# Retention's scores and transposes as quarter-array products, two pacing constants, and the order of the last retention step

## The chip, the cores and the metric

The kernel runs on one core of a Trainium2 chip. The metric is the device time of one execution in microseconds. TensorE does the matrix products, VectorE and ScalarE empty its result banks, GpSimd does a few elementwise steps, SyncE issues most transfers.

## What is computed

Three layers follow each other: a retention over 4 batches of 8 heads with 576 positions and head size 64, then a layer with a mish-like gate (512 to 2048 to 512), then a layer with a SiLU gate (512 to 1536 to 512). Tokens: 4 x 576 = 2304.

```python
scores = scale * np.matmul(q, k.transpose(0, 1, 3, 2))
Dmat = np.where(rel >= 0, gamma[:, None, None] ** rel[None, :, :], 0.0)
ret = scores * Dmat[None, :, :, :]
attn = np.matmul(ret, v)
...
h = x @ w_in
sp = np.where(h > 20.0, h, np.log1p(np.exp(np.minimum(h, 20.0))))
x = (h * np.tanh(sp)) @ w_out
...
g = x @ w_gate
silu = g * (1.0 / (1.0 + np.exp(-g)))
out = (silu * (x @ w_val)) @ w2_out
```

## The kernel before, in words

Every engine executes its instructions in the order in which the program writes them.

**Retention** (`retention`, lines 441 to 799) runs 20 steps: four batches, each of four chunks of 128 positions and one of 64. In a step `scores` (line 601) multiplies keys by queries into the bank tile `s`, one product for each of 8 heads; VectorE multiplies by the mask into `p` (line 616). Then `turn` (line 509) transposes what the next steps need: the keys of the next step (`k_item`) and a part of the queries of a later one (`q_item`, chosen by `q_next`). ScalarE copies the results out of the bank. Then `output` (line 672) adds three things: the carried state times queries (line 685), the update of the state (`state`, line 650) and masked scores times scaled values (line 700). ScalarE copies the state out (`state_out`, line 664) and VectorE multiplies the output by a decay into `x` (line 713). In eight of the steps (`EARLY`) `g1` puts one product of the next layer (line 808, bank `h`) between line 685 and line 650.

A head has 64 columns, so these products fill a part of the array of 128 rows and 128 columns. The trace gives the part as rows*columns: scores stand as 64*128 (two in the array at a time, one for each half of the rows), line 685 as 64*64 (four at a time), lines 650 and 700 as 128*64 (two at a time). The transposes come in two kinds. `halves` (line 493) uses the transpose operation on 64 rows and 128 columns, one product for each; `quarters` (line 499) multiplies by the identity on 64 rows and 64 columns, and the trace shows two products for each such call, as it does for all other float32 calls of this stage. Keys need quarters for odd pairs of heads, full query chunks (`whole`) use halves alone. The chunk of 64 positions uses only the upper half of the rows. At the start of batch 0 the queries of steps 2 and 3 are transposed inside step 1 (`q0_1` by ScalarE, `q0_1b` by VectorE).

**First gated layer** (lines 1139 to 1189). For the last part `pair1` runs seven block products for each of eight pairs of columns, twice. The block products of one pair share two banks, emptied by ScalarE and VectorE; the line of a block product is 965, the line of the second matmul that is put between them is 1020. Beside this, `second`, a `Pace` object (line 396), emits the preparation of the third layer's weights (VectorE lines 133, 137, 228, 238, 276, with ScalarE casts and transfers). Each call adds a rate to an allowance and emits pieces while the allowance covers their costs. `RATES[2]` is the rate in the middle of a run, `RATES[4]` the rate of the last eleven block products. What is left at the end is emitted at once by `second(1000.0)`, ahead of the second gated layer (`strassen`, line 1243), whose block products use line 965 too, in tile `t`.

Of the kernel before, what the change touches and what calls it, by code (L numbers as in the profile page):

```python
# [17 lines left out]
def retention_mish_swiglu(  # L18
# [17 lines left out]
    nc = tc.nc  # L36
# [5 lines left out]
    NP = H // 2  # L42
# [4 lines left out]
    RAW, XS = 4, 6  # L47
    W = (12, 3, 3)
    NC = 2
    RATES, AHEAD = (0.8, 1.2, 1.37, 0.95, 1.05), 45  # L50
    EARLY = (8, 10, 11, 13, 14, 16, 17, 19)
    FIRSTS = (0, 2, 1, 3, 4, 5, 6, 7)
    REST, NO_FETCH = (1, 3, 6, 18), (2, 5)
# [381 lines left out]
    steps = []  # L435
# [5 lines left out]
    def retention(g1, mish, g_hi, g_lo):  # L441
        with ExitStack() as c0:
# [6 lines left out]
            ident = cp.tile([128, 128], F32, tag="ident", name="ident")  # L449
# [33 lines left out]
            qT, kT, vs, pp = {}, {}, {}, {}  # L483
# [5 lines left out]
            def row(pr, e):  # L489
                r = 64 * (e ^ pr % 2)  # L490
                return slice(r, r + 64)

            def halves(n, src, to, pairs):
                for pr in pairs:
                    for r in range(-(-n // 64)):
                        own = slice(64 * r, min(64 * r + 64, n))
                        nc.tensor.transpose(to(r, pr)[:, :own.stop - own.start], src(pr)[own], ident[own, own])  # L497

            def quarters(n, src, to):
                for pr in range(1, NP, 2):  # L500
                    for e in range(2):
                        for r in range(-(-n // 64)):
                            own = slice(64 * r, min(64 * r + 64, n))
                            nc.tensor.matmul(  # L504
                                to(r, pr)[row(pr, e), :own.stop - own.start], lhsT=src(pr)[own, e, :],
                                rhs=ident[own, own], start=True, stop=True, skip_group_check=True,
                            )

            def turn(name, *items, tag="tt", both=False):
                items = [x for x in items if x]  # L510
                if not items:
                    return
                p = ps1.tile([128, 2, 2, NP, 64], F32, tag=tag, name=f"t{name}")
                to = [lambda r, pr, z=z: p[:, r, z, pr] for z in range(2)]
                for z, (n, src, _, whole) in enumerate(items):
                    halves(n, src, to[z], range(0, NP, 1 if whole else 2))
                for z, (n, src, _, whole) in enumerate(items):
                    if not whole:
                        quarters(n, src, to[z])
                for z, (_, _, empty, _) in enumerate(items):  # L520
                    if not both:
                        empty(p[:, :, z])
                        continue
                    for r, copy in enumerate((nc.scalar.copy, nc.vector.tensor_copy)):
                        empty(p[:, :, z], r, copy)


            def first_k():
                n, src, *_ = k_item(0)
                p = [ps1.tile([128, NP, 64], F32, tag=tag, name=f"tk0_{tag}") for tag in ("o", "st")]  # L530
                halves(n, src, lambda r, pr: p[r][:, pr], range(0, NP, 2))
                quarters(n, src, lambda r, pr: p[r][:, pr])
                kT[0] = at.tile([128, NP, 128], F32, tag="kT", name="kT0")
                for r, copy in enumerate((nc.scalar.copy, nc.vector.tensor_copy)):
                    copy(out=kT[0][:, :, 64 * r:64 * r + 64], in_=p[r])
# [43 lines left out]
            def q_cols(t):  # L579
                b, sc, n = steps[t]  # L580
                return qT[b, sc // 2][:, :, sc % 2 * 128:sc % 2 * 128 + n]
# [19 lines left out]
            def scores(t):  # L601
                b, sc, n = steps[t]
                s = ps1.tile([128, 2, NP, 128], F32, tag="s", name=f"s{t}")
                for pr in range(NP):
                    for e in range(2):
                        nc.tensor.matmul(  # L606
                            s[:n, e, pr, :n],
                            lhsT=kT[t][64 * e:64 * e + 64, pr, :n],
                            rhs=q_cols(t)[64 * e:64 * e + 64, pr],
                            start=True,  # L610
                            stop=True,
                        )
                pp[t] = at.tile([128, 2, NP, 128], F32, tag="p", name=f"p{t}")
                for c in range(2):
                    own = slice(c * NP // 2, (c + 1) * NP // 2)
                    nc.vector.tensor_tensor(
                        out=pp[t][:n, :, own, :n],
                        in0=s[:n, :, own, :n],
                        in1=mask[:n, :n].unsqueeze(1).unsqueeze(1).to_broadcast([n, 2, NP // 2, n]),
                        op=ALU.mult,  # L620
                    )
# [37 lines left out]
            def state_out(t):  # L659
                b, sc, n = steps[t]  # L660
                if sc == nsc - 1:
                    return
                if sc < nsc - 2:
                    nc.scalar.copy(out=sd, in_=stp[b])
                    return
                for e in range(2):
                    for m in range(2):
                        nc.scalar.copy(
                            out=sbd[row(m, e), m::2, 64 * e:64 * e + 64], in_=stp[b][row(m, e), m::2, :],
                        )  # L670

            def output(t):
                b, sc, n = steps[t]

                o = ps1.tile([128, 2, 512], F32, tag="o", name=f"o{t}")
                o = o.rearrange("p b (a n) -> p b a n", n=128)

                def place_of(pr, e):
                    return o[64 * e:64 * e + 64, pr % 2, pr // 2, :n]

                if sc:
                    for pr in range(NP):
                        for e in range(2):
                            own = row(pr, e)
                            nc.tensor.matmul(  # L685
                                place_of(pr, e),
                                lhsT=sd[own, pr, :] if n == 128 else sbd[:, pr, 64 * e:64 * e + 64],
                                rhs=q_cols(t)[own, pr] if n == 128 else q_cols(t)[:, pr],
                                start=(pr < 2), stop=False, skip_group_check=True,
                            )  # L690
                if t in EARLY:
                    g1(FIRSTS[EARLY.index(t)])
                state(t)
                if t == 1:
                    turn("q0_1", q_item(0, 1, 0))
                    turn("q0_1b", q_item(0, 1, 1, nc.vector.tensor_copy), tag="s")
                state_out(t)
                for pr in range(NP):
                    for e in range(2):
                        nc.tensor.matmul(  # L700
                            place_of(pr, e),
                            lhsT=vs[t][:n, 2 * pr + e, :],
                            rhs=pp[t][:n, e ^ pr % 2, pr, :n],
                            start=(sc == 0 and pr < 2), stop=True, skip_group_check=True,
                        )
                t0 = b * S + sc * 128
                done = 0
                while done < n:
                    j, off = divmod(t0 + done, T)
                    m = min(n - done, T - off)  # L710
                    if j not in xt:
                        new_x(xt, j, "x")
                    nc.vector.tensor_tensor(
                        out=xt[j][:, :, off:off + m].rearrange("p (a b) n -> p b a n", b=2),
                        in0=o[:, :, :NP // 2, done:done + m],
                        in1=gout[:, :, sc * 128 + done:sc * 128 + done + m].rearrange("p (a b) n -> p b a n", b=2),
                        op=ALU.mult,
                    )
                    done += m
                    if j < 2 and off + m == T:  # L720
                        due.extend((j, kk) for kk in range(KT))
# [79 lines left out]
    with tc.manual_schedule():  # L801
# [15 lines left out]
        def g1(s):  # L817
            i, b = divmod(s, NC)
            hs[s] = h_bank(f"h{s}")
            prod(hs[s], unit["in", i], "x", b)  # L820
# [326 lines left out]
        for i in range(inside, F1):  # L1147
            for b in range(NC):
                s = NC * i + b
# [270 lines left out]
        for k, (load, steps_) in enumerate(more):  # L1420
            side[0, 2 * k, 0, 6 * k] = [load]
            if k == 0:
                at_ = [(0, 1, 0, c) for c in range(NG)] + [(0, 1, 1, c) for c in range(4)] + [(0, 2, 0, c) for c in range(3)]
# [76 lines left out]
```

## Time and profile before

| what | value |
|---|---|
| median of three runs | 878.18 us (878.05 to 879.94) |
| the profiled execution's own time | 878.28 us |
| its span (first to last instruction) | 876.5 us |
| TensorE busy | 869.0 us, 99% of the span |
| VectorE busy | 641.6 us, 73% |
| ScalarE busy | 429.7 us, 49% |
| GpSimd busy | 48.6 us, 6% |

The span and the 1.8 us around it make the profiled time. Retention fills the first 102 us of the span, the first gated layer reaches to about 464 us. In the timeline a row is a group of neighbouring instructions of one line; its first number is when the first of them starts, its second how long the group lasts, and the ends of matmuls are modelled, so the text takes differences between starts.

### The profile page before, as it was taken

How to read it: one execution, taken by the hardware profiler on the slowest of the kernel's cores; microseconds unless marked ns; L12 is line 12 of the kernel's file. 1: busy time of each engine (PE TensorE's matmuls, PEld its weight loads, DVE VectorE, ACT ScalarE, POOL GpSimd, SP SyncE). 2: the span in 40 equal slices, each digit the busy share in tenths (PEclk: the TensorE clock that was granted, in tenths of full speed). 3: DMA queues.
4: the chain of work that ended last, by engine and by line, in shares of the span. 5: the costliest groups of instructions: out<-in, count | busy, mean ns of one | idle time of the engine just before them, and what ended most of it. 6: DMA issues, size and time to landing. Idle time of an engine off the chain costs nothing.

```text
span 876.5 us, 17164 instructions
## 1 busy us (share of the span) xinstructions
PE 869.0 (99%) x6570; PEld 830.4 (95%) x6570; DVE 641.6 (73%) x1260; ACT 429.7 (49%) x842; POOL 48.6 (6%) x46
## 2 busy tenths in 40 slices
PE   8999999999999999999999999999999999999998
PEld 8888899999999999999998999999999999999998
DVE  4678688887887876878695877975676776575773
ACT  3667367776665655656664342363222263222260
POOL 3554200000000000000000000000000000000000
PEclk9999999999999999999999999999999999999999
DMA  9999647886799985999977799878877878777773
GB/s 214 227 252 222 204 138 261 284 319 214 246 341 315 333 288 189 313 340 335 305 272 282 257 359 306 276 248 297 272 250 248 249 255 285 279 252 249 248 248 128
DMA packets 162850, 232.25 MB, mean 265 GB/s; under 512 B 48336, under 2 KB 126672, under 8 KB 162768
## 3 DMA queue, kind: packets, MB, share of 16 engines
q1 hardware_dynamic: 161232, 230.33, 81.7%
q8 instruction: 52, 0.85, 0.4%
q10 hardware_dynamic: 1536, 0.82, 0.4%
q14 instruction: 30, 0.25, 0.1%
HBM read 178.68 MB, written 52.43 MB: 264 GB/s over the span
## 4 chain that ended last, share of the span: by engine, by line
PE 92%; DVE 4%; DMA 2%; ACT 1%; issue 1%; SPq 0%; POOL 0%; DVEq 0%; ACTq 0%; POOLq 0%
PE t L965 30%; PE T L1386 15%; PE te L965 12%; PE h L808 8%; PE e0a L1020 8%; PE pa L1020 8%; PE e1a L1020 5%; PE s L606 2%; PE o L700 2%; PE state L650 1%; DMA v<-in_v_dram 1%; PE t L504 1%; DMA fcomb<-c 1%; PE o L685 1%; DVE y L920 1%; PE t L497 1%
## 5 line engine op out<-in xcount | busy, mean ns | idle before, releaser
L965 PE MATMUL t<-y,su 128*128 128x384 f32 x1512 | 267.9, 337 | 1.1 <-DVE scratch L972 0.8
L965 PEld LDWEIGHTS t<-y,su 128*128 128x128 f32 x1512 | 264.1, 188 | 3.5 <-DVE scratch L972 1.1
L965 PE MATMUL te<-ye,eu 128*128 128x384 f32 x672 | 135.9, 337 | 0.0
L1386 PE MATMUL T<-su,g 128*128 128x256 f32 x1134 | 135.3, 282 | 0.0
L1386 PEld LDWEIGHTS T<-su,g 128*128 128x128 f32 x1134 | 135.2, 190 | 0.0
L965 PEld LDWEIGHTS te<-ye,eu 128*128 128x128 f32 x672 | 113.1, 188 | 4.7
L1020 PE MATMUL e1a<-ge,u 128*128 128x512 f32 (+1 forms) x384 | 76.1, 337 | 0.0
L1020 PE MATMUL e0a<-ge,u 128*128 128x512 f32 (+1 forms) x384 | 76.1, 337 | 0.0
L808 PE MATMUL h<-xs,u 128*128 128x384 f32 x384 | 72.8, 338 | 0.0
L1020 PE MATMUL pa<-g,u 128*128 128x512 f32 (+1 forms) x384 | 72.2, 336 | 0.0
L1020 PEld LDWEIGHTS e1a<-ge,u 128*128 128x128 f32 x384 | 61.9, 188 | 6.0
L1020 PEld LDWEIGHTS e0a<-ge,u 128*128 128x128 f32 x384 | 62.0, 188 | 5.9
L808 PEld LDWEIGHTS h<-xs,u 128*128 128x128 f32 x384 | 65.3, 188 | 2.1 <-issue 0.9
L1020 PEld LDWEIGHTS pa<-g,u 128*128 128x128 f32 x384 | 60.5, 188 | 6.7
L1255 ACT ACTIVATE sg<-sg 128x384 f32<-128x384 f32 x54 | 28.4, 526 | 57.3 <-DVE sg L972 57.3
L1284 ACT COPY p<-t 128x384 f32<-128x384 f32 x35 | 16.6, 473 | 81.0 <-PE t L965 81.0
L1216 ACT CAST g<-ga 128x384 fp32r<-128x384 f32 x72 | 32.6, 517 | 44.1 <-DVE ga L1263 33.4
L972 DVE TENSOR_TENSOR u<-t,p 128x384 f32<-128x384 f32 x36 | 20.1, 557 | 40.9 <-PE t L965 40.9
L975 DVE TENSOR_TENSOR g<-ga,g 128x384 fp32r<-128x384 f32 x72 | 36.2, 551 | 6.4 <-ACT g L1216 6.2
L972 DVE TENSOR_TENSOR scratch<-te,scratch 128x384 f32<-128x384 f32 x48 | 26.6, 554 | 7.6 <-PE te L965 4.3
L972 DVE TENSOR_TENSOR v<-t,p 128x384 f32<-128x384 f32 x36 | 20.1, 557 | 15.9 <-PE t L965 15.8
L1063 ACT ACTIVATE ve<-ve 128x384 f32<-128x384 f32 x16 | 8.4, 527 | 45.7 <-DVE ve L972 45.7
(194 smaller groups left out, 1190.1 us busy)
## 6 DMA issues: line engine op xcount, KB each, us to landing
su<-comb SPq DMA_DIRECT2D x126, 512.0 KB, 4.3
su<-fcomb SPq DMA_DIRECT2D x63, 512.0 KB, 4.3
eu<-ecomb SPq DMA_DIRECT2D x56, 512.0 KB, 5.8
comb<-c SPq DMA_DIRECT2D x48, 256.0 KB, 5.2
raw<-in_moe_w_in_dram SPq DMA_DIRECT2D x16, 512.0 KB, 5.2
raw<-in_moe_w_out_dram SPq DMA_DIRECT2D x16, 512.0 KB, 5.7
ecomb<-e SPq DMA_DIRECT2D x32, 256.0 KB, 4.7
ecomb<-u SPq DMA_DIRECT2D x24, 256.0 KB, 4.6
```

The costliest lines, as they stand in the source:

```text
L497: nc.tensor.transpose(to(r, pr)[:, :own.stop - own.start], src(pr)[own], ident[own, own])
L606: nc.tensor.matmul(s[:n, e, pr, :n], lhsT=kT[t][64 * e:64 * e + 64, pr, :n], rhs=q_cols(t)[64 * e:64 * e + 64, pr], start=True, stop=True,)
L700: nc.tensor.matmul(place_of(pr, e), lhsT=vs[t][:n, 2 * pr + e, :], rhs=pp[t][:n, e ^ pr % 2, pr, :n], start=(sc == 0 and pr < 2), stop=Tru ...
L808: nc.tensor.matmul(ps, lhsT=u[:, a, kk * 128:(kk + 1) * 128], rhs=s[:, e, :], start=(c == 0), stop=(c == n - 1),)
L965: nc.tensor.matmul(p, lhsT=w[:, (high, 1 - high)[a], kk * 128:(kk + 1) * 128], rhs=y[kk][:, x, :], start=begin and kk == 0 and (a, x) == ( ...
L972: nc.vector.tensor_tensor(out=out_, in0=a, in1=b_, op=ALU.add)
L975: nc.vector.tensor_tensor(out=out_, in0=a, in1=b_, op=ALU.subtract)
L1020: nc.tensor.matmul(o, lhsT=unit["out", f][:, a, d * 128:(d + 1) * 128], rhs=y[:, :512] if r == 0 else y[:, 512:], start=f == 0 and (a, x) ...
L1216: nc.scalar.copy(out=gt[n, c, i][:, 0], in_=x)
L1255: nc.scalar.activation(x, bank_ if part_ is None else x, AF.Silu)
L1284: (nc.scalar.copy if n or i or z else nc.vector.tensor_copy)(out=r["p1"], in_=p)
L1386: nc.tensor.matmul(p[m], lhsT=g[:, x, m * 128:(m + 1) * 128], rhs=w[:, 1 - a, :], start=begin and i == 0 and (a, x) == (0, 0) and not (sha ...
```

## The change

Three edits. Scores are cut into pieces of 64 key columns, so that four stand in the array at a time, and all transposes are quarters; the function for halves is gone. In the last of the 20 steps `g1` comes ahead of the state's products; in step 1 `state_out` is written behind line 700's products. Two rates of the pacing change.

```diff
-    RATES, AHEAD = (0.8, 1.2, 1.37, 0.95, 1.05), 45
+    RATES, AHEAD = (0.8, 1.2, 1.42, 0.95, 0.95), 45
...
-            def halves(n, src, to, pairs):
-                for pr in pairs:
-                    for r in range(-(-n // 64)):
-                        own = slice(64 * r, min(64 * r + 64, n))
-                        nc.tensor.transpose(to(r, pr)[:, :own.stop - own.start], src(pr)[own], ident[own, own])
-
-            def quarters(n, src, to):
-                for pr in range(1, NP, 2):
+            def quarters(n, src, to, whole):
+                for pr in range(NP):
                     for e in range(2):
+                        at_ = slice(64 * e, 64 * e + 64) if whole else row(pr, e)
                         for r in range(-(-n // 64)):
                             own = slice(64 * r, min(64 * r + 64, n))
                             nc.tensor.matmul(
-                                to(r, pr)[row(pr, e), :own.stop - own.start], lhsT=src(pr)[own, e, :],
+                                to(r, pr)[at_, :own.stop - own.start], lhsT=src(pr)[own, e, :],
                                 rhs=ident[own, own], start=True, stop=True, skip_group_check=True,
                             )
...
                 for z, (n, src, _, whole) in enumerate(items):
-                    halves(n, src, to[z], range(0, NP, 1 if whole else 2))
-                for z, (n, src, _, whole) in enumerate(items):
-                    if not whole:
-                        quarters(n, src, to[z])
+                    quarters(n, src, to[z], whole)
...
                 for pr in range(NP):
-                    for e in range(2):
-                        nc.tensor.matmul(
-                            s[:n, e, pr, :n],
-                            lhsT=kT[t][64 * e:64 * e + 64, pr, :n],
-                            rhs=q_cols(t)[64 * e:64 * e + 64, pr],
-                            start=True,
-                            stop=True,
-                        )
+                    for c in range(0, n, 64):
+                        for e in range(2):
+                            nc.tensor.matmul(
+                                s[c:c + 64, e, pr, :n],
+                                lhsT=kT[t][64 * e:64 * e + 64, pr, c:c + 64],
+                                rhs=q_cols(t)[64 * e:64 * e + 64, pr],
+                                start=True, stop=True, skip_group_check=True,
+                            )
...
+                if t + 1 == len(steps):
+                    g1(FIRSTS[EARLY.index(t)])
                 if sc:
...
-                if t in EARLY:
+                if t in EARLY and t + 1 < len(steps):
                     g1(FIRSTS[EARLY.index(t)])
                 state(t)
...
-                state_out(t)
+                if t != 1:
+                    state_out(t)
...
+                if t == 1:
+                    state_out(t)
```

The orders below give instructions by line, written tile, read tiles and output size; a call counts once, and line numbers behind the edits are lower by 4 to 9 in the changed kernel.

On TensorE, step 6, a full chunk with keys (`k`) and a whole query part (`q`) to transpose, before:

```order
L606 MATMUL s_709<-qT_0_521,kT_671 128x128 x8
L497 MATMUL t_721<-ident,k_563 128x64 x4
L497 MATMUL t_721<-ident,q_488 128x64 x8
L504 MATMUL t_721<-ident,k_563 64x64 x8
L685 MATMUL o_751<-qT_0_521,sd 64x128 x8
L650 MATMUL state_680<-vs_676,k_490 64x64 x8
```

And the same step of the changed kernel:

```order
L598 MATMUL s_833<-qT_0_613,kT_795 64x128 x16
L499 MATMUL t_853<-ident,k_655 64x64 x16
L499 MATMUL t_853<-ident,q_562 64x64 x16
L678 MATMUL o_895<-qT_0_613,sd 64x128 x8
L641 MATMUL state_804<-vs_800,k_564 64x64 x8
```

Eight score calls become 16, and 12 halves with 8 quarters become 32 quarters; from the scores to line 685 all calls have one shape of tile.

On TensorE, the last step (scores `s`, the layer's product `h`, the state's part and the rest of the output `o`), before:

```order
L606 MATMUL s_1791<-qT_2_1655,kT_1752 64x64 x8
L685 MATMUL o_1804<-qT_2_1655,sbd 64x64 x8
L808 MATMUL h_1813<-xs_0_853,u_1256 128x384 x3
L808 MATMUL h_1813<-xs_1_943,u_1256 128x384 x3
L808 MATMUL h_1813<-xs_2_1022,u_1256 128x384 x3
L808 MATMUL h_1813<-xs_3_1111,u_1256 128x384 x3
L700 MATMUL o_1804<-p_1800,vs_1754 64x64 x8
```

And now:

```order
L598 MATMUL s_2127<-qT_2_1975,kT_2088 64x64 x8
L804 MATMUL h_2141<-xs_0_1011,u_1498 128x384 x3
L804 MATMUL h_2141<-xs_1_1119,u_1498 128x384 x3
L804 MATMUL h_2141<-xs_2_1210,u_1498 128x384 x3
L804 MATMUL h_2141<-xs_3_1319,u_1498 128x384 x3
L678 MATMUL o_2140<-qT_2_1975,sbd 64x64 x8
L694 MATMUL o_2140<-p_2136,vs_2090 64x64 x8
```

The 12 products of `h` stand between the scores and the state's part, which is now followed at once by the rest of the output.

On VectorE, the end of the first gated layer, behind its last-but-one block product (`scratch` and `ge` belong to the block products, `y` to the next layer's input, `c` and `rawf` to the weights that `second` prepares, `p_0_0` to the next layer's first block product), before:

```order
L920 TENSOR_TENSOR y_5_1_5601<-t_0_5424,y_5_1_5601 128x384
L228 TENSOR_TENSOR c_0_5529<-c_0_5529 128x512
L972 TENSOR_TENSOR scratch<-te_7_3_5560,scratch 128x384
L1070 TENSOR_TENSOR ge_15_5571<-scratch,ge_15_5571 128x384
L920 TENSOR_TENSOR y_6_0_5606<-y_3116,y_6_0_5606 128x384
L920 TENSOR_TENSOR y_6_1_5607<-y_3116,y_6_1_5607 128x384
L228 TENSOR_TENSOR c_1_5556<-c_1_5556 128x512
L228 TENSOR_TENSOR rawf_0_5323<-rawf_0_5323 128x256
L1284 COPY p_0_0_5663<-t_0_0_1_5656 128x384
```

And now:

```order
L916 TENSOR_TENSOR y_5_1_5947<-t_0_5771,y_5_1_5947 128x384
L968 TENSOR_TENSOR scratch<-te_7_3_5909,scratch 128x384
L1066 TENSOR_TENSOR ge_15_5920<-scratch,ge_15_5920 128x384
L916 TENSOR_TENSOR y_6_0_5952<-y_3452,y_6_0_5952 128x384
L916 TENSOR_TENSOR y_6_1_5953<-y_3452,y_6_1_5953 128x384
L1280 COPY p_0_0_5999<-t_0_0_1_5992 128x384
```

The three pieces of line 228 stand earlier now, ahead of the addition `ve_7` of the fifth block product of that pair. On the queue of SyncE the transfers of prepared weights and of `su` and `eu` tiles are moved past each other in the same stretch.

## Rows read from the trace of the kernel before

**Rows 1.** The page: busy us, share of the span, instructions of each engine.
```profile
PE 869.0 (99%) x6570; PEld 830.4 (95%) x6570; DVE 641.6 (73%) x1260; ACT 429.7 (49%) x842; POOL 48.6 (6%) x46
```

**Rows 2.** TensorE's waits: who waited for whom, total us, times, longest.
```profile
PE t L965 <- DVE scratch L972: 0.8, 1, 0.8
...
PE o L700 <- DVE p L616: 0.3, 1, 0.3
```

**Rows 3.** Timeline, TensorE, step 6: start, us, engine, line, tiles, array part, output, count.
```profile
33.74 1.16 PE L606 MATMUL s<-qT,kT 64*128 64x128 f32 x16
34.73 0.28 PE L497 MATMUL t<-ident,k 64*128 64x64 f32 x4
...
35.20 0.46 PE L504 MATMUL t<-ident,k 64*64 64x64 f32 x16
35.48 0.62 PE L685 MATMUL o<-qT,sd 64*64 64x128 f32 x16
36.03 0.69 PE L650 MATMUL state<-vs,k 128*64 128x64 f32 x16
```

**Rows 4.** Timeline, TensorE, step 12: keys, then the short query chunk.
```profile
64.36 0.29 PE L497 MATMUL t<-ident,k 64*128 64x64 f32 x4
...
64.98 0.35 PE L504 MATMUL t<-ident,q 64*64 64x64 f32 x6
...
65.21 0.61 PE L685 MATMUL o<-qT,sd 64*64 64x128 f32 x14
```

**Rows 5.** Timeline, TensorE, step 13: short key chunk, then a whole query part.
```profile
68.24 0.22 PE L497 MATMUL t<-ident,k 64*128 64x64 f32 x1
...
68.98 0.61 PE L685 MATMUL o<-qT,sd 64*64 64x128 f32 x14
```

**Rows 6.** Timeline, TensorE, step 14, a chunk of 64 positions.
```profile
73.29 0.68 PE L606 MATMUL s<-qT,kT 64*64 64x64 f32 x16
73.90 0.34 PE L497 MATMUL t<-ident,k 64*128 64x64 f32 x4
...
74.81 0.69 PE L685 MATMUL o<-qT,sbd 128*64 128x64 f32 x16
```

**Rows 7.** Timeline, step 1's query transposes and their copies, then step 2.
```profile
15.82 0.46 PE L497 MATMUL tq<-ident,q 64*128 64x64 f32 x8 [0.16 <-DMA q<-in_q_dram]
...
16.46 1.09 PE L700 MATMUL o<-p,vs 128*64 128x128 f32 x16
16.57 1.40 DVE L554 COPY qT<-tq_1b 64x512 f32<-64x512 f32 x2 [1.14 <-PE tq_1b L497]
...
18.11 1.16 PE L606 MATMUL s<-qT,kT 64*128 64x128 f32 x16 [0.55 <-ACT sd L664]
...
19.51 0.34 PE L497 MATMUL t<-ident,q 64*128 64x64 f32 x2
```

**Rows 8.** Timeline, TensorE, the last step: scores and the state's part.
```profile
97.53 0.68 PE L606 MATMUL s<-qT,kT 64*64 64x64 f32 x16
98.48 0.69 PE L685 MATMUL o<-qT,sbd 128*64 128x64 f32 x16 [0.27 <-DVE x L713]
```

**Rows 9.** Timeline, end of the first gated layer, TensorE and one row of VectorE.
```profile
460.16 1.20 PE L1020 MATMUL e1a<-ge,u 128*128 128x512 f32 x6
...
462.26 1.21 PE L1020 MATMUL e1a<-ge,u 128*128 128x512 f32 x6
...
463.68 0.55 DVE L972 TENSOR_TENSOR scratch<-te,scratch 128x384 f32<-128x384 f32 x1
...
464.28 1.32 PE L965 MATMUL t<-y,su 128*128 128x384 f32 x6 [0.81 <-DVE scratch L972]
...
465.44 1.61 PE L1020 MATMUL e1a<-ge,u 128*128 128x512 f32 x8
...
468.25 1.56 PE L1020 MATMUL e1a<-ge,u 128*128 128x512 f32 x8
```

**Rows 10.** Timeline, VectorE, a piece of `second` that waits for a transfer.
```profile
438.38 0.43 DVE L238 TENSOR_TENSOR c<-c,rawf 128x256 f32<-128x256 f32 x1 [1.81 <-DMA fcomb<-c]
```

More of the change, by code (lines that the diff above doesn't have):

```diff
@@ L530, in first_k @@
                 p = [ps1.tile([128, NP, 64], F32, tag=tag, name=f"tk0_{tag}") for tag in ("o", "st")]
-                halves(n, src, lambda r, pr: p[r][:, pr], range(0, NP, 2))
-                quarters(n, src, lambda r, pr: p[r][:, pr])
+                quarters(n, src, lambda r, pr: p[r][:, pr], False)
                 kT[0] = at.tile([128, NP, 128], F32, tag="kT", name="kT0")
```

## The prediction

> **What bounds the kernel now.** I read three views in this order. The page first: TensorE is busy for 869.0 of 876.5 us [rows 1], so a change counts only by what it does to TensorE's own work or to its few waits. Then the list of TensorE's waits: little stands in it, and the two rows that touch this change are 0.8 us of line 965 for a VectorE addition and 0.3 us of line 700 for masked scores [rows 2]. Last the timeline of single retention steps, where the reader should look at the distances from one row's start to the next: they repeat to 0.01 us from step to step, since TensorE is seldom waited out. Retention is therefore a sum of TensorE pieces, and the change replaces pieces.
>
> **The paces.** All sums rest on four numbers.
> - A set of products with 64 output columns costs 0.058 us, whether two or four stand in the array: 8 products of a short query chunk, two abreast, take 0.23 us from 64.98 to 65.21 [rows 4].
> - Four sets of four take 0.28 us from 35.20 to 35.48 [rows 3], which is 4 x 0.058 and 0.05 for the start after the tile form has changed.
> - A set with 128 output columns costs 0.11 us in either form: scores take 0.99 us for 8 sets of two, line 685 takes 0.55 us for 4 sets of four [rows 3], and the difference is four sets.
> - Halves cost 0.03 us each, and a change of form 0.10 us: 12 halves take 0.47 us from 34.73 to 35.20 [rows 3].
>
> **Scores.** Cutting them in two doubles the products (16 to 32) and the number abreast, so there are still 8 sets. What is saved is the longer start: 0.99 becomes 8 x 0.11 + 0.05 = 0.93, that is -0.06 in each of 16 full steps, -1.0 together. In the short chunks nothing is cut, but the following transposes have the same form now: 0.61 [rows 6] becomes 8 x 0.058 + 0.05 = 0.51, three times -0.10.
>
> **Transposes.** A call of `halves` is one product for a 64x128 block; as quarters it is four products. The keys' and whole queries' transposes of a step (0.75 us from 34.73 to 35.48 [rows 3]) become 64 products in 16 sets of 0.058, 0.93 us: +0.18 in six steps, +1.1. Steps with a short query chunk (0.85 us, 64.36 to 65.21 [rows 4]) also come to 0.93: +0.08, four times, +0.3. Steps with a short key chunk (0.74 us, 68.24 to 68.98 [rows 5], and 0.01 of line 685 that ran under it) come to 0.93 and lose that overlap: +0.20, three times, +0.6. Behind a chunk of 64 (0.91 us, 73.90 to 74.81 [rows 6]) it is 0.93 and one change of form, 0.10: +0.13, three times, +0.4. Keys alone get 0.03 cheaper (0.12 + 0.10 + 0.28 against 0.47) in two steps and at the head. The query transposes of step 1 (0.64 us, 15.82 to 16.46 [rows 7]) are 16 halves; as 64 products with start and change of form they take 1.09, +0.45, and the same pattern stands once more at the head: +0.9. Together the transposes cost +3.2, and scores and transposes +1.9 us of TensorE time.
>
> **What hides some of it.** In step 1 the transposes wait for a query load (0.16 us [rows 7]), so about 0.2 us of what came before costs nothing. Step 2's scores do not wait for TensorE but for the copies of step 1's transposes: VectorE starts them at 16.57, takes 1.40, and scores start at 18.11 [rows 7]. With the transposes 0.45 later this wait stays and all moves by 0.45, as summed. In step 2 the short query chunk's transposes start at 19.51, some 0.3 later than 18.11 + 0.99 + 0.12, waiting for a load; the longer key transposes now fill that. In steps 5 and 6 line 700 waits for VectorE's masking (0.3 us [rows 2] and shorter ones beside it), which takes +0.12 of each. Sum hidden: 0.75 us. If a load came later than here, its wait would return and the cover be smaller.
>
> **The last step.** Scores run from 97.53 and the state's part starts at 98.48, 0.95 us later, because VectorE still reads the output bank [rows 8]; the same 16 products take 0.61 before the next row in step 14 [rows 6]. With the next layer's 12 products in between, that 0.34 us goes. They write another bank and wait for nothing that is late there. Moving step 1's `state_out` changes the order on no engine (ScalarE copies the same things in the same order): 0.
>
> Retention thus becomes 1.9 - 0.75 - 0.34 = +0.8 us longer.
>
> **The pacing.** Before the second gated layer TensorE runs 6 and 6 products in 2.10 us (460.16 to 462.26), 0.175 each. The next 12 take 3.18 (to 465.44), the 14 after them 2.81 instead of 2.45 (to 468.25): 1.08 + 0.36 = 1.44 us lost [rows 9]. The row at 464.28 names the cause: it needs a bank that VectorE's addition at 463.68 frees, over 3 us after its block product, and the order shows weight pieces of line 228 in front of that addition and of the copy behind it. The new rates emit 0.05 more in each of 73 calls and 0.1 less in each of the last 11 (counted in the code of `pair1`), 2.55 units of allowance earlier, so these pieces lie ahead of the last three block products. VectorE has idle time earlier to take them (it even stood 1.81 us for a transfer at 438 [rows 10]). I take -1.3 of the 1.44; bounds are 0 and -1.44.
>
> **Sum.** 878.28 + 0.8 - 1.3 = 877.8 us by the profiled execution, which stands 0.10 above the median of the runs, so **877.7 us**. Its own range, from a set at 0.055 instead of 0.058 (half of a 128-column set; 288 sets, -0.9) and from hidden time that is not hidden (+0.75), is 876.7 to 878.7.
>
> **Rivals.** 0.2% or 1.8 us is about what a measurement of this kernel can tell from no change.
> - **The pacing frees nothing**: the addition is as late as before because ScalarE's casts lead to it. Retention alone remains: 879.0. Against it stands that three pieces are gone from the front of that queue. Chance 0.16.
> - **Quarters are cheaper than read**: sets at 0.055, the whole 1.44 us back, and the retention's added time filling more of the small waits: 877.7 - 0.9 - 0.14 - 0.4 = 876.2. Chance 0.19.
> - **VectorE stands for a transfer at a worse time** (slower): pieces that come earlier relative to TensorE find the write of their predecessor not landed and hold the in-order queue, as at 438.38 for 1.81 us [rows 10]. TensorE can stand a late addition of about 3.1 us, from the end of the block product near 460.2 to 463.3, where the bank is wanted [rows 9]; a stand decides when it pushes one beyond that. Price: no gain and 1.2 us more, 878.18 + 0.8 + 1.2 = 880.2. For it: VectorE waits for transfers here already. Against: the slower last rate gives slack at the end. Chance 0.13.
> - **Small products are not supplied fast enough** (slower): no row shows more than 16 of the four-abreast 64-column products in a run, now there are up to 64. If those past the first 16 go at the pace of two abreast, 0.029 instead of 0.0145 each, some 690 products cost +10: 888. Against it: 16 products leave in 0.28 us, 0.0175 each with the start included, with 16 of line 685 close behind [rows 3]. Chance 0.05. [...]
>
> **How the numbers follow.** The forecast has 0.47. Faster by over 0.2% (below 876.4) is the third case alone, 0.19; slower (above 879.9) the last two, 0.18; the forecast and idle pacing make 0.63 within. The range 876.0 to 880.2 takes in all but the slow supply and the outer parts of the two cases at its ends, under 2 in 10.
>
> **What would show it.** Right: in the changed trace step 6's scores take 0.93 from start to start and its transposes 0.93; line 1020, which ends retention, starts 0.8 later than before; the 0.8 us row of line 965 is gone from the waits. Wrong: transposes at 1.5 us or more in a step (supply), scores under 0.85 (four abreast better than read), a new wait of lines 965 or 1020 for VectorE in the first gated layer (pacing).

## The result and the profile after

The changed kernel takes **890.44 us** (median of six runs, 888.46 to 892.43) against 878.29 us for the kernel before beside it: a ratio of 1.0135, with a 95% interval of 1.0114 to 1.0155, so it is slower by some 12 us. (One of the six executions before took 1205.73 us, far outside all others, and is not in the ratio.) The forecast was 877.7 us with a range to 880.2. The profiled execution took 891.62 us with a span of 889.8, 13.3 more than the span before.

The page of the changed kernel, TensorE's busy time and the queues of transfers (packets, MB, share of the 16 transfer engines). In the kernel before, queue q8 carried 52 packets and 0.85 MB.

```profile
PE 873.8 (98%) x7450; PEld 836.2 (94%) x7450; DVE 638.5 (72%) x1260; ACT 429.9 (48%) x842; POOL 48.9 (5%) x46
...
q1 hardware_dynamic: 161232, 230.33, 80.3%
q8 instruction: 59, 0.97, 0.5%
```

TensorE has 880 products more than before ([rows 1]: 6570), each with a weight load of its own. Its busy time grew by only 4.8 us, so most of the 13.3 us is time in which it stands. The list of its waits (engine line, released by: us in total, times, longest) says where:

```profile
PE t L499 <- issue: 8.0, 6, 1.9
...
PE tq L499 <- issue: 0.8, 1, 0.8
PE s L598 <- ACT qT L545: 0.7, 2, 0.4
PE s L598 <- issue: 0.7, 2, 0.3
PE s L598 <- DVE qT L545: 0.6, 1, 0.6
```

The wait of 0.8 us for VectorE's addition [rows 2] is gone, as forecast. New are the rows "issue": waits for no engine and no transfer that the view knows. The timeline shows two steps of the same 64 products. Step 11:

```profile
70.03 1.10 PE L598 MATMUL s<-qT,kT 64*64 64x128 f32 x32
70.95 0.65 PE L499 MATMUL t<-ident,k 64*64 64x64 f32 x32
71.42 0.65 PE L499 MATMUL t<-ident,q 64*64 64x64 f32 x32
71.88 0.62 PE L678 MATMUL o<-qT,sd 64*64 64x128 f32 x16
72.43 2.35 PE L804 MATMUL h<-xs,u 128*128 128x384 f32 x12
74.71 0.69 PE L641 MATMUL state<-vs,k 128*64 128x64 f32 x16
```

Scores take 0.92 us from start to start, transposes 0.93, to a hundredth what the prediction summed against [rows 3]. And step 8, where the queries' transposes stop in the middle:

```profile
49.23 1.10 PE L598 MATMUL s<-qT,kT 64*64 64x128 f32 x32
50.15 0.57 PE L499 MATMUL t<-ident,k 64*64 64x64 f32 x13
...
50.61 0.52 PE L499 MATMUL t<-ident,q 64*64 64x64 f32 x16
52.90 0.40 PE L499 MATMUL t<-ident,q 64*64 64x64 f32 x11 [1.77 <-issue]
...
53.73 3.91 PE L804 MATMUL h<-xs,u 128*128 128x384 f32 x12
57.57 0.68 PE L641 MATMUL state<-vs,k 128*64 128x64 f32 x16
```

All instructions of TensorE are counted here from the start of the program: products, weight loads and the 259 waits and drains that stand between them. By this count the stops lie at 449, 705, 961, 1217, 1473 and so on: always a multiple of 256 apart (remainder 193). The waits and drains belong to it, although the recorded expectations speak of products and loads alone: without them the remainder of the stops of line 499 slides from 185 at 17.55 to 167 at 65.63. One packet of q8 has 16,384 bytes. Behind the first 193, the 15,159 instructions of the changed kernel make 58.5 times 256, where q8 has 59 packets; before, 13,399 make 51.6 and there are 52. So a packet of q8 is **256 of TensorE's instructions**, and TensorE stands where one packet ends and the next is not there. For the stop at 50.9 the view of transfers shows it: from 46.8, when the packet in use was entered, to 50.4 q8 has no packet, and in the next 1.3 us it has one, beside 691 of the data queue q1:

```profile
q1 hardware_dynamic: 691, 0.29, 98.9%
q8 instruction: 1, 0.02, 5.5%
```

It landed at 51.61 and TensorE resumed at 52.90. In retention the next packet starts 1.2 to 3.7 us after the one before was entered, takes 0.9 to 1.3 us, and at the stops TensorE resumes 1.2 to 1.6 us after it landed (q8's records against TensorE's).

A second loss follows the same stop. The granted clock, by windows (us, then busy times of five engines, clock, transfer share, GB/s):

```profile
44.00:53.80 9.80, 8.03 (x255) 7.20 (x250) 5.45 (x9) 5.32 (x13) 5.52 (x5) 1.00 0.85 215
53.80:57.20 3.40, 3.40 (x11) 3.40 (x12) 0.00 (x0) 1.11 (x2) 0.00 (x0) 0.50 0.81 196
57.20:66.00 8.80, 6.99 (x239) 6.04 (x239) 5.85 (x10) 4.94 (x13) 5.22 (x5) 1.00 0.87 226
```

For 3.4 us the granted clock is 0.50 instead of 1.00, and line 804's twelve products take 3.84 us (53.73 to 57.57) instead of the 2.28 that they take in step 11 (72.43 to 74.71), at a granted clock of 1.00.

**The balance.** Line 1016, which ends retention, starts at 116.78; its counterpart before, line 1020, started at 101.99. The first row is of before, the second of the changed kernel:

```profile
101.99 8.59 PE L1020 MATMUL pa<-g,u 128*128 128x512 f32 x48
116.78 8.60 PE L1016 MATMUL pa<-g,u 128*128 128x512 f32 x48
```

That is +14.79. Twelve gaps of more than 0.3 us at packet ends (from the last start before to the first start after) make 12.66; before there was one, 0.41: +12.25. The clock costs 1.56. What is left, +0.98, is close to the prediction's own sum for retention, +0.8; it is a remainder, so it also holds what the stands hid or added of other waits. From there to the last product the changed kernel is 1.45 faster (769.52 against 770.97): 14.79 - 1.45 = 13.34.

### The profile page after: what moved, and what is told of

Same layout as the page of the kernel before. It is cut to its first block, busy times and chain, and to the rows that moved or that the text cites. A ratio compares the mean times of both kernels' runs of the same rounds, so it can differ in the third digit from the quotient of the medians.

```text
span 889.8 us, 18918 instructions
## 1 busy us (share of the span) xinstructions
PE 873.8 (98%) x7450; PEld 836.2 (94%) x7450; DVE 638.5 (72%) x1260; ACT 429.9 (48%) x842; POOL 48.9 (5%) x46
## 4 chain that ended last, share of the span: by engine, by line
PE 97%; issue 1%; DVE 1%; ACT 0%; ACTq 0%; DVEq 0%
PE t L961 29%; PE T L1382 15%; PE te L961 13%; PE h L804 8%; PE e0a L1016 8%; PE e1a L1016 8%; PE pa L1016 8%; PE s L598 2%; PE t L499 2%; PE o L694 2%; PE state L641 1%; PE o L678 1%; PE idle L741 1%; ACT qT L545 0%; PE tq L499 0%
## 5 line engine op out<-in xcount | busy, mean ns | idle before, releaser
L971 DVE TENSOR_TENSOR g<-ga,g 128x384 fp32r<-128x384 f32 x72 | 36.2, 551 | 6.4 <-ACT g L1212 6.2
L709 DVE TENSOR_TENSOR x<-o,gout 128x512 f32<-128x512 f32 (+1 forms) x22 | 12.9, 593 | 28.7 <-PE o L694 28.6
L833 DVE TENSOR_TENSOR g<-m,g 128x384 fp32r<-128x384 f32 x32 | 19.4, 608 | 16.7 <-ACT g L828 16.6
```

Source lines behind the costliest of these rows:

```text
L833: nc.vector.tensor_tensor(out=g[:, 1, b], in0=ws.pop(s), in1=g[:, 0, b].bitcast(F32), op=ALU.subtract)
L971: nc.vector.tensor_tensor(out=out_, in0=a, in1=b_, op=ALU.subtract)
```

## Experiments

Theories: (1) TensorE's instructions come in packets of 256, only the next one is fetched, and a stretch that uses 256 faster than that stands; (2) the stands belong to transposes, their data or their place in a step; (3) on top of (1), data transfers make the packets late. The retention ends and the stands below are taken from one profile of each kernel, as in the balance above.

### The pacing alone

```diff
-    RATES, AHEAD = (0.8, 1.2, 1.37, 0.95, 1.05), 45
+    RATES, AHEAD = (0.8, 1.2, 1.42, 0.95, 0.95), 45
```

> The kernel before with the change's two pacing rates alone. Both theories of retention leave it untouched, so this prices the pacing by itself. If the prediction's step holds, the 0.8 us row of line 965 goes from TensorE's waits and the time falls by 1.3 us (bounds 0 and 1.44): 876.9. If pacing frees nothing: 878.3. If VectorE stands for a transfer instead: 879.5. TensorE's instructions are those of before, so no new stand in retention.

878.13 us, ratio 0.9996 (0.9987 to 1.0005): not told from before, and the forecast gain of 1.3 us (0.9985) lies just outside the interval. In the profile the wait is gone and the part behind retention is 1.07 us shorter (769.90), while retention ended 0.55 later, at 102.54, with TensorE waiting 1.0 us for one load of queries. In this profile the stage gained; the whole time does not show it. In eight profiles with the new rates the part behind retention takes 769.5 to 770.0 in seven (771.84 in one, below); in three with the old rates 770.97, 771.54 and 770.26. So behind retention the new rates are mostly ahead, by 0.3 to 2 us. The size goes with the wait for VectorE's addition that the old rates leave: 1.1 us in the profile with 771.54, 0.8 in that with 770.97, and no wait that the view lists in that with 770.26.

### Scores in quarters alone

```diff
-                    for e in range(2):
-                        nc.tensor.matmul(
-                            s[:n, e, pr, :n],
...
+                    for c in range(0, n, 64):
+                        for e in range(2):
+                            nc.tensor.matmul(
+                                s[c:c + 64, e, pr, :n],
...
```

> The kernel before with scores in quarters alone; 32 more TensorE instructions (products and weight loads) in a full step, 216 instead of 184. Theory 1 (TensorE's instructions come in packets of 256, the next one can be had only some 4.1 to 6.2 us after the one before was entered): 256 instructions are now about 4.7 us of work, so some packet ends are waited for, 0 to 1.5 us each at up to half of some 16, all at places 256 instructions apart: 1.3 saved, 2 to 5 lost, 879 to 882. Rival (the stands belong to the transposes, or to data that they read): the prediction's sum, -1.3, 877.0, and no stand.

880.09 us, ratio 1.0017 (1.0008 to 1.0026). The time is inside theory 1's range, but not for its reason: the profile has only one stand at a packet end, 1.13 us. The loss is where I had expected a gain:

```profile
35.56 1.10 PE L607 MATMUL s<-qT,kT 64*64 64x128 f32 x32
36.60 0.34 PE L497 MATMUL t<-ident,k 64*128 64x64 f32 x4
...
37.12 0.46 PE L504 MATMUL t<-ident,k 64*64 64x64 f32 x16
```

Scores and halves take 1.04 + 0.52 = 1.56 us (35.56 to 37.12) instead of 1.46 [rows 3]: halves behind quarters pay a change of form that halves behind the old scores did not. 16 steps of 0.10 are 1.6. Scores in quarters pay here only when what follows has the same form (0.92 in step 11).

### Transposes in quarters alone

The change with the scores, the rates and the last step of before (edits as in the change's diff, the other way).

> The change with the scores, the rates and the last step of before: the transposes in quarters alone, 256 TensorE instructions in a full step, about 4.1 us of work without the next layer's product. Theory 1: stands at nearly every packet end of a step without that product, each some 0.45 us shorter than in the changed kernel, together 6 to 8 us, with 2.4 for the transposes 885 to 889. Rival (the stands belong to the transposes and their data): the same eight long transposes as in the changed kernel, 12 us of stands, 891 to 892. By the prediction's own sum without any stand: 880.7.

890.68 us, ratio 1.0139 (1.0124 to 1.0155), above theory 1's range. The stands at packet ends make 7.07 us, as expected; the clock fell once (0.50 from 27.6 to 31.0), and old scores ahead of quarters take 1.09 us (20.34 to 21.43) instead of 0.99, 1.6 us in 16 steps that I had left out. The rival falls by the place of the longest stand:

```profile
20.34 1.16 PE L597 MATMUL s<-qT,kT 64*128 64x128 f32 x16 [0.57 <-DVE qT L545]
21.43 0.69 PE L499 MATMUL t<-ident,k 64*64 64x64 f32 x32
...
23.47 0.60 PE L692 MATMUL o<-p,vs 128*64 128x128 f32 x7
26.59 0.71 PE L692 MATMUL o<-p,vs 128*64 128x128 f32 x9 [2.52 <-issue]
```

It lies between the seventh and the eighth of 16 products of line 692, no transposes, at count 961, remainder 193.

### The program moved against the packets

```diff
-    W = (12, 3, 3)
+    W = (28, 3, 3)
```

> The change with 16 more warming products at its head, 64 more TensorE instructions (products and weight loads) ahead of retention, some 7 us of added time. Theory 1 (packets of 256 instructions): the stands stay at the same counts, 256 apart with the remainder 193 when products and loads are counted from the start, and so move to other places in the program, 64 instructions earlier; the total of stands stays within 9 to 15 us. Rival (waits for data or for a place in the step): the stands stay at the same products of the same steps, that is at counts 64 higher, remainder 1.

887.76 us (one time). All stands of more than 0.3 us that name no engine keep the remainder 193 and so lie at other products. Their total, 6.8 us, is below the range I gave, and the clock never fell. The added products also start retention 4.0 us later (its first transposes at 10.50 instead of 6.48), so this run does not tell whether the smaller total comes from where the packet ends fall or from the later start. A second shift, with 8 warming products instead of 16:

> The change with 8 more warming products at its head, 32 more TensorE instructions. Theory 1: stands at counts of remainder 193 again, their total between those of the changed kernel (12.7 us) and of the shift by 64 (6.8 us) or near either, since it hangs on which products a packet end meets; time 885 to 892. Rival (places in the program): remainder 225.

888.67 us (one time), remainder 193 again, stands of 10.3 us. One of them, a gap of 2.19 us at 37.6 us, lies where the count is 1729; at that count the unshifted kernel has a gap of 0.33:

```profile
39.81 0.68 PE L499 MATMUL t<-ident,q 64*64 64x64 f32 x28 [1.97 <-issue]
```

Theory 2 falls: the count decides where TensorE stands, not the place in the program. How much is lost differs by 6 us between the three profiles (12.7, 10.3, 6.8), each of a single execution; the times of the unshifted kernel alone spread over 4 us, so what share the alignment has is not shown.

### Fewer transfers

```diff
+                old = 4 if nm == "k" else 3
+                if old <= t < len(steps):
+                    qkv[nm, t] = qkv[nm, t % old]
...
```

> The change without the key loads past the first four steps and the value loads past the first three: later steps use the earlier tiles again, so their keys and values are not the input's. Some 450 KB less traffic in a step. Theory 3 (the instruction packet waits behind data on the transfer engines): the packet starts within 1 us of the entry into the one before instead of 1.2 to 3.7 us, stands shrink from about 13 us to under 6, time about 883. Theory 1 alone, with a fixed delay: delays and stands as in the changed kernel, 10 to 13 us, 888 to 891.

882.41 us, ratio 1.0079 (1.0012 to 1.0146), from three times: 882.30, 882.41 and 888.59. The third lies among the changed kernel's own times (its mean granted clock is 0.996, theirs 0.996 to 1.000) and has no profile, so the reading rests on the profile, which is that of 882.30. There the stands shrink to 5.3 us, no clock falls, and retention ends at 107.43 instead of 116.78. The waits:

```profile
PE t L502 <- issue: 2.9, 3, 1.3
...
PE tq L502 <- issue: 0.8, 1, 0.8
```

Up to 50 us packets still start up to 2.9 us after the entry, with 0.9 to 1.0 MB of the data that is left moved in the two longest of these delays, and the stands are there; from 54 us on they start within 1.1 us of the entry and nothing stands, although TensorE's instructions are the same. That is theory 3.

### The fetch by itself

```python
for i in range(calls):
    e, r = i % 2, i // 2 % 2
    nc.tensor.matmul(p[64 * e:64 * e + 64, r, i // 4 % 8], lhsT=src[64 * r:64 * r + 64, 64 * e:64 * e + 64], ...)
```

> The whole computation is left out: zeros are written. In its place 2560 calls of the 64x64 form, four abreast, 4 instructions each (two products, two weight loads), 10240 in all: first 640 calls with no transfer beside them, then 960 beside a stream of loads with 2 KB rows, then 960 beside loads of keys with 256-byte rows. By its own pace (0.058 us for four products) a packet of 256 instructions is 1.9 us of work. Theory 1: a stand every 256 instructions, the packet period well above 1.9 us even without other transfers (packet 1.0 to 1.3 us and 1.2 to 1.6 from its landing to the next product: 2.5 to 3 us). Theory 3: the period grows to 4 us or more beside the streams, most beside the short rows. If the supply were no limit: 1.9 us per 256 in all three.

The timeline, first without transfers (up to some 19 us the zeros were still being written), then beside the 2 KB rows, without transfers again, and beside the 256-byte rows:

```profile
27.63 2.09 PE L50 MATMUL quiet<-src 64*64 64x64 f32 x128 [1.91 <-issue]
31.36 2.09 PE L50 MATMUL quiet<-src 64*64 64x64 f32 x128 [1.64 <-issue]
34.81 2.09 PE L50 MATMUL quiet<-src 64*64 64x64 f32 x128 [1.36 <-issue]
...
42.00 2.09 PE L50 MATMUL rows<-src 64*64 64x64 f32 x128 [1.36 <-issue]
47.65 3.54 PE L50 MATMUL rows<-src 64*64 64x64 f32 x128 [3.56 <-issue]
53.29 2.90 PE L50 MATMUL rows<-src 64*64 64x64 f32 x128 [2.11 <-issue]
...
92.72 2.09 PE L50 MATMUL rows<-src 64*64 64x64 f32 x128 [1.36 <-issue]
96.44 2.09 PE L50 MATMUL rows<-src 64*64 64x64 f32 x128 [1.64 <-issue]
...
116.18 3.42 PE L50 MATMUL heads<-src 64*64 64x64 f32 x128 [3.28 <-issue]
120.73 2.09 PE L50 MATMUL heads<-src 64*64 64x64 f32 x128 [1.14 <-issue]
125.28 3.16 PE L50 MATMUL heads<-src 64*64 64x64 f32 x128 [2.46 <-issue]
```

Every group is 128 products, with their loads 256 instructions. From start to start it is 3.45 to 3.73 us without other transfers (31.36, 34.81), 5.65 us beside the 2 KB rows (42.00, 47.65, 53.29; 4.8 to 6.2 over all), 3.72 again once they are over (92.72, 96.44), and 4.55 beside the short rows (116.18, 120.73, 125.28; 3.7 to 5.4). A group of 2.09 us (its last product ends 0.22 after its start) is the pace without a limit, 1.87. Without traffic a packet starts 1.0 to 1.2 us after the one before was entered, beside the 2 KB rows 2.3 to 3.8 and beside the short rows 1.2 to 2.6. The windows show the traffic beside it: 4, 367, 5 and 206 GB/s.

```profile
22.00:38.00 16.00, 8.46 (x519) 7.83 (x512) 0.00 (x0) 0.00 (x0) 1.00 0.02 4
44.00:85.00 41.00, 22.28 (x903) 21.06 (x896) 0.18 (x1) 0.00 (x0) 0.71 1.01 367
90.00:107.00 17.00, 9.72 (x606) 9.05 (x596) 0.00 (x0) 0.00 (x0) 1.00 0.02 5
112.00:170.00 58.00, 36.17 (x1694) 34.28 (x1687) 0.99 (x2) 0.00 (x0) 0.79 0.96 206
```

Theories 1 and 3 both hold here. The granted clock is lower beside the streams (0.71 and 0.79 in the mean), but slower products are not what lengthens the period: TensorE still stood before every packet there, for some 0.5 us at the least. My 2.5 to 3 us for the quiet part was too short by the 1.0 to 1.2 us before a packet starts. The guess that short rows hurt most was wrong: the 2 KB rows, with more bytes at about the same share of the transfer engines (1.01 and 0.96), delay a packet more.

### Quarters only in long steps, and only in short ones

```diff
+    FINE = lambda t: t in EARLY
...
+                size = 64 if FINE(t) else n
...
-                turn(f"{t + 1}", k_item(t + 1), q_next(t), both=t in BOTH)
+                turn(f"{t + 1}", k_item(t + 1), q_next(t), both=t in BOTH, fine=FINE(t))
```

> The two rates and the last step of the change, with scores and transposes in quarters only in the eight steps that hold a product of the next layer. Some 312 TensorE instructions in such a step, but it lasts 6.3 us, so 256 are 5.2 us of work. Theory 1 (256 instructions to a packet, one packet ahead): few stands at packet ends, 0 to 2 us together, no fall of the clock from them; by the prediction's sums the quarters cost about 0.6 us in these steps, the rates and the last step give 1.5: 877.2 without a stand, up to 879.5 with. Rival (these products cost the stands wherever they are): 8 of 20 steps, about 5 of the 12.7 us, 882.

880.62 us, ratio 1.0021 (1.0010 to 1.0032). Stands at packet ends 1.9 us, inside theory 1's 0 to 2, and only 1.3 of them in a step with quarters (the other 0.6 at 29.38, in a step without); the clock holds. The time is 1.1 above its range. The ten times lie between 878.61 and 881.73, and the profile is one of the longer ones (881.64 us). What it lost elsewhere it names: loads that came late (0.4 to 1.1 us in three rows), and a wait of the prediction's third rival, at another place. VectorE stands for a transfer, and TensorE then for VectorE:

```profile
309.71 0.43 DVE L239 TENSOR_TENSOR c<-rawg 128x256 f32<-128x256 f32 x1 [3.57 <-DMA comb<-c]
...
310.66 1.32 PE L972 MATMUL te<-ye,eu 128*128 128x384 f32 x6 [1.63 <-DVE scratch L979]
```

The complement, `t not in EARLY`:

> The complement: quarters only in the twelve steps that hold no product of the next layer, 256 to 288 TensorE instructions in about 4 us. Theory 1: most of the changed kernel's stands at packet ends, 6 to 11 us, all 256 instructions apart; with 1.5 from rates and last step, some 0.6 for the quarters and perhaps 1.5 for a fall of the clock 884 to 889. Rival (the same cost in each step with quarters): 12 of 20 steps, about 7.5 us, 885, and no difference by the step's length.

884.07 us, ratio 1.0070 (1.0055 to 1.0085), with stands of 6.52 us and one fall of the clock (from 32.8 to 36.2). Stands at packet ends per step with quarters: 0.2 us in the eight long ones, 0.5 in the twelve short ones. That is theory 1's direction; the rival, the same cost in every step with quarters, asked for some 5 us in the long ones. The second run alone fits the rival's 7.5 us and 885 as well; it is the first that speaks against it. All long steps come late, from step 8 on, but that alone does not spare them: in the same part of the changed kernel, which has quarters in the short steps 9, 12, 15 and 18 too, the stands make 5.2 us.

### The two other edits alone

Rates and last step of the change, everything else as before (edits as in the change's diff).

> The kernel before with the two rates and the last step's first product moved ahead of the state's part, no quarter added: TensorE's instruction count is that of before. Theory 1: no stand in retention beyond before's, 1.3 to 1.4 from the pacing and 0.34 from the last step, 876.5. If the move of the product is worth nothing: 876.9; if it makes the mish of that product or the next line wait: 877.2 or more.

877.65 us, ratio 0.9993 (0.9984 to 1.0002): the fastest median of all, but not told from before, and the expected 876.5 (0.9981) lies outside the interval. The step itself does what was summed:

```profile
101.00 0.68 PE L606 MATMUL s<-qT,kT 64*64 64x64 f32 x16
101.61 2.35 PE L810 MATMUL h<-xs,u 128*128 128x384 f32 x12
103.89 0.69 PE L687 MATMUL o<-qT,sbd 128*64 128x64 f32 x16
```

0.61 us from scores to the layer's products, where 0.95 stood before the state's part [rows 8]. The 3 us later than in the kernel before are this execution's own (880.21 us): one load of keys came 1.7 us late at 43 us and the clock fell behind it, and one packet end was waited for (1.1 us).

## Why the prediction was wrong

**The step that failed** is the first: "Retention is therefore a sum of TensorE pieces". It holds while the pieces are there to be executed. The sum priced 1760 more instructions by their pace in the array and left out that they must be fetched. A step without a product of the next layer had about 184 instructions in 4 us before; 256 then last 5.6 us, and the packets kept up with one exception. With 288 they last 3.5 us, about what a packet takes with no other traffic at all (3.45 to 3.73) and less than the 4 to 6 us beside retention's loads. What the runs showed in place of the plain sum is 12.25 us of stands at packet ends and 1.56 of slower clock behind one of them.

A sign lay in the trace of before: a stand of 0.4 us in the middle of line 650, at count 1473, remainder 193. I read only the rows that named an engine. In the timeline of the kernel before:

```profile
40.18 0.34 PE L650 MATMUL state<-vs,k 128*64 128x64 f32 x4
40.70 0.51 PE L650 MATMUL state<-vs,k 128*64 128x64 f32 x11 [0.19 <-issue]
```

Point by point:

- **Paces**: right, 0.92 and 0.93 us a step where nothing stands. What is left of retention's +14.79 without the stands and the clock is +0.98, forecast +0.8.
- **Last step**: right, 0.34.
- **Pacing**: -1.45 measured behind retention, forecast -1.3. But alone it did not move the whole time, and 1.3 lies outside that run's interval; the size was in part luck.
- **Small products not supplied fast enough** (888, chance 0.05): right in kind, and near in time only by accident. Its mechanism, 0.029 us for each product past the sixteenth, did not come about: 64 products run at 0.0145 each in step 11. The supply failed in lumps, at counts 256 instructions apart. The sign that the prediction named for it, transposes of 1.5 us or more in a step, did come, in the steps with a stand (step 8: from 50.15 to past 52.90). The chance was too small because I tested the rival on 16 products, which lie inside one packet.
- **Where the packets kept up**: packets that last 5 us and more were there in time for the most part, with single stands left (0.4 us before; 1.1 with the two other edits, where the packet started only 5.0 us after the entry). Those of some 3.5 us mostly were not: in the changed kernel TensorE stood for more than 0.3 us at twelve packet ends, 12.66 us together.
- **Without a forecast**: the clock's fall after a stand, 1.56 us.

What stays open: why a packet starts more than a microsecond after the one before was entered even without traffic, and on which of the 16 transfer engines it queues; the records don't tell.

## What to carry to other kernels

Count instructions as well as array time: products, weight loads and waits of a stretch, divided by 256, give the packets that it needs, and each took 3.5 to 3.7 us in quiet and 3.7 to 6.2 us beside heavy transfers here. Splitting products into smaller ones that fill the array better brings more instructions in the same time: here TensorE stood for its packets where 256 last 3.5 us by their pace (12.25 us more in retention), and with one exception did not where they last 5.6 us. So put such products beside long ones: the stands came to 0.2 us in a long step with quarters and 0.5 in a short one. A wait that names no engine, in the middle of equal products, is to be counted from the start of the program before anything else is believed about it.

## What the hardware showed that I had not expected

- TensorE resumed only 1.2 to 1.6 us after the instruction packet that it stood for had landed, at all twelve stops of the changed kernel, and 1.5 us after it at the one stop of the kernel before.
- Of six stands of 1.8 us or more in retention, four were followed within 0.6 to 1.3 us of their end by 3.4 us at a granted clock of 0.50 (after the stands that ended at 52.90 in the changed kernel, 26.59 with the transposes alone, 31.55 with quarters in short steps and 45.09 in the kernel with the two other edits, where the stand was for a load); two of 2.15 and 2.19 us were not. The stand of 1.99 us thus cost 1.56 more.
- With four 64 by 64 tiles abreast, 64 products took 0.93 us in step 11, one each 14.5 ns, and 128 took 1.87 us in the fetch by itself, one each 14.6 ns, where their instructions were there.
